# A new order for the down stages of a mixture-of-experts kernel: rows' sums, weights' pairs, output copies and gathers

## The chip, the cores and the metric

The kernel runs on one core of a Trainium2 chip. The metric is the device time of one execution in microseconds; the median of three runs is given. The engines are called TensorE (PE in the profile's rows; its weight loads are PEld), VectorE (DVE), ScalarE (ACT), GpSimd (POOL) and SyncE (SP, which only issues DMAs). A name like L1277 is a line of the kernel before.

## The reference

First comes causal attention with decay: 8 batches of 8 heads, 576 positions, 64 dimensions. Its output, as 4608 rows of 512 numbers, goes through a mixture of 8 experts. Each row is given to the expert with the largest gate logit; the expert computes `relu(x @ w1[e]) @ w2[e]` (512 to 1024 to 512), and the result is scaled by the row's gate weight and by a sigmoid of a second gate.

```
e_idx = argmax(x @ w_gate)
for e in range(8):
    rows = e_idx == e
    out[rows] = gate_w * eom[e] * (relu(x[rows] @ w1[e]) @ w2[e])
```

## The kernel before

The attention runs in the first 330 us by an order written out by hand; the change leaves it alone. Its rows go to DRAM as float16 upper and lower parts. The experts follow, in another hand-written order (`manual_schedule`): every engine runs its instructions in the order in which the code issues them. An instruction that waits holds up all that stands behind it on its engine.

**Numbers in two parts.** A float32 matrix is held as an upper float16 part and a lower part; a product is three matmuls: upper with upper, upper with lower, lower with upper.

**One expert.** Each expert has a fixed room for rows: two with 640, the others with 640, 608, 592, 576, 560 and 512 (`CAPS`). An expert has an up stage (`up_seven`) and a down stage (the loop over tiles at the end of `expert`'s code). The up stage multiplies by a seven-product scheme of Strassen's kind on halves: the weights are used as A11, A12, A22, S1, S2, S4, S3 and the rows as four quarters of `xT` and four sums T1 to T4. For each of four pairs `p` of weight blocks it forms products in three PSUM tiles: `y` (in a bank named `hp0`), `z` and `v` (banks `hp1`). A product that is used twice is first copied by ScalarE to `keep` (L1290), and the next product is then accumulated onto it in the same bank. VectorE adds the pieces (L1314, L1318, L1324); ScalarE and VectorE write the upper and the lower part of the hidden rows (`hh` L1282, `hl` L1284). The seventh product of the last pair (`finish_up`) runs inside the first tile of the down stage.

**The down stage** makes one output tile of 128 rows after another (`down_sum`, L1091 to L1093, 24 matmuls of 512 columns into a bank `y`; there are two such banks). ScalarE copies the bank, scaled, to `ys` (L1103), and GpSimd scatters `ys` to the output by an indirect DMA (L1107). A last tile with 96 rows or fewer is *narrow*: its matmuls take 64 or 32 rows side by side (`narrow_sum`, L1124), and VectorE adds the partial sums up (L1132, L1134; six instructions when it has both a 64-row and a 32-row part, two when it has 64 rows only).

**Prepared in the shadow of these stages, for the next expert:**

- The rows are gathered from DRAM by GpSimd's indirect DMAs (`gather_rows`, L816, one per tile of 128) and turned by DMA transposes on SyncE's queue (`gather_turn`, L822). Both are issued in `between`, which is called eight times in an up stage (`fc` 0 to 7).
- `between` also splits one W2 tile of this expert: ScalarE makes the upper part (L1009), GpSimd the lower part (L1010). It fetches the W2 tile four further on, and from `fc` 4 on tiles of the next W1 (L778).
- `rows_whole` adds upper and lower part of the turned rows to float32 (L1235): four GpSimd instructions over all columns, behind the up stage.
- `rows_sums` makes T1 to T4 for one half `k` of the contraction: VectorE subtracts into PSUM tiles in `hp1` (L1247), ScalarE casts the upper part (L1248), VectorE subtracts for the lower part (L1251). It is called in the second and the third tile of a down stage.
- `weights_pair` makes the seven blocks of one pair of W1: VectorE forms S1, S2, S4 (L1208, L1210, L1211) and two lower parts, GpSimd forms S3 in the tile `xr` (L1209) and three lower parts (L1206), ScalarE casts the upper parts (L1203). It is called in tiles 0, 1, 3 and 4, before that tile's output copy.

So on ScalarE the order within one tile is: sums (tiles 1 and 2), pair (all but tile 2), output copy of the tile.

**The hand-over** from attention to experts (from 349 us) is written out separately. The first expert (`W2`, `h`) has three tiles early and two (`xl`) later; in between, all of the second expert's rows are gathered and turned, its four W1 pairs are made without GpSimd (`first_splits`), and its sums follow the up stage of the two late tiles (L1065). On SyncE's queue the order is: transposes of `xl`, four fetches of W2 tiles, five transposes of `x1`. On the side engines: both halves of the sums, the last pair, then the two tiles with their copies.

## Time and profile before

| | us |
|---|---|
| median of 3 runs | 731.97 (728.39 to 734.08) |
| the profiled execution | 736.71 |
| its span, first to last instruction | 735.0 |
| TensorE busy | 690.8 |
| GpSimd busy | 554.6 |
| VectorE busy | 514.5 |
| ScalarE busy | 415.4 |

The profile is of one execution. Busy time leaves out the instructions that only wait, branch or issue a DMA. A wait of an engine is put down to the instruction, or the DMA, whose end came last before it went on.

The stages on this time line: attention to 330, hand-over to 386.5, then seven experts, each an up stage of 19 to 30 us and a down stage of 24 to 28 us, and an end of about 7 us after the last matmul.

### The profile page before, as it was taken

How to read it: one execution, taken by the hardware profiler on the slowest of the kernel's cores; microseconds unless marked ns; L12 is line 12 of the kernel's file. 1: busy time of each engine (PE TensorE's matmuls, PEld its weight loads, DVE VectorE, ACT ScalarE, POOL GpSimd, SP SyncE). 2: the span in 40 equal slices, each digit the busy share in tenths (PEclk: the TensorE clock that was granted, in tenths of full speed). 3: DMA queues.
4: the chain of work that ended last, by engine and by line, in shares of the span. 5: the costliest groups of instructions: out<-in, count | busy, mean ns of one | idle time of the engine just before them, and what ended most of it. 6: DMA issues, size and time to landing. Idle time of an engine off the chain costs nothing. (4 is left out here: it accounts for less than half of the span.)

```text
span 735.0 us, 22266 instructions
## 1 busy us (share of the span) xinstructions
PE 690.8 (94%) x8823; PEld 457.4 (62%) x8842; DVE 514.5 (70%) x1175; ACT 415.4 (57%) x990; POOL 554.6 (75%) x618
## 2 busy tenths in 40 slices
PE   4999999999999989989997999999989899889996
PEld 1577777777777767776464646547447356475664
DVE  7567798899889977876845575575585585656642
ACT  4456676667667645654425556566456465665641
POOL 8779799999989987862534768778767777788742
PEclk9999999999999999999998999999999999999999
DMA  4536666677797575265763934917819529366201
GB/s 153 162 115 175 176 169 168 167 170 165 191 178 188 158 164 140 61 139 179 195 127 93 220 124 121 273 60 171 225 46 207 195 69 246 130 145 230 76 15 40
DMA packets 119451, 110.71 MB, mean 151 GB/s; under 512 B 82669, under 2 KB 92077, under 8 KB 119344
## 3 DMA queue, kind: packets, MB, share of 16 engines
q1 hardware_dynamic: 108566, 71.50, 40.7%
q10 hardware_dynamic: 4618, 18.88, 8.6%
q0 software_dynamic: 6160, 18.88, 8.0%
q8 instruction: 70, 1.15, 0.7%
q14 instruction: 37, 0.30, 0.2%
HBM read 72.47 MB, written 19.49 MB: 125 GB/s over the span
## 5 line engine op out<-in xcount | busy, mean ns | idle before, releaser
L434 POOL TENSOR_TENSOR plo<-p 128x512 f16<-128x512 f32 x182 | 194.5, 1087 | 25.9 <-PE mx L305 12.7
L1277 PE MATMUL hp<-xT,sh 128*128 128x320 f16 (+5 forms) x784 | 150.8, 292 | 11.5 <-ACT keep L1290 7.9
L336 DVE TENSOR_REDUCE nR<-mx 128x2 f32<-128x1024 f32 (+4 forms) x154 | 121.2, 804 | 39.5 <-PE mx L305 37.2
L432 ACT ACTIVATE p<-sc 128x512 f32<-128x512 f32 x192 | 111.5, 595 | 65.3 <-PE sc L305 63.2
L305 PE MATMUL sc<-qk 64*128 64x64 f32 (+5 forms) x644 | 114.8, 435 | 0.0
L1277 PE MATMUL hp<-xT,sl 128*128 128x320 f16 (+5 forms) x392 | 114.4, 292 | 0.0
L1091 PE MATMUL y<-w2h,hh 128*128 128x512 f16 x272 | 103.1, 379 | 7.6 <-ACT ys L1103 7.6
L1093 PE MATMUL y<-w2h,hl 128*128 128x512 f16 x272 | 103.1, 379 | 1.0
L1277 PEld LDWEIGHTS <-sh 128*128 128x128 f16 x784 | 77.1, 99 | 39.1 <-issue 15.1
L1092 PE MATMUL y<-w2l,hh 128*128 128x512 bf16 x253 | 95.9, 379 | 0.0
L305 PEld LDWEIGHTS <-pick 64*128 64x128 bf16 (+1 forms) x1152 | 55.4, 98 | 56.2 <-issue 43.0
L1010 POOL TENSOR_TENSOR w2l<-w2r,w2h 128x512 bf16<-128x512 f32 x56 | 65.0, 1163 | 31.4 <-ACT w2h L1009 30.1
L505 PE MATMUL av<-Vs,p 128*128 128x65 f16 x640 | 65.8, 193 | 1.3 <-ACT xr L552 1.3
L1282 ACT ACTIVATE hh<-hp 128x320 f16<-128x320 f32 (+5 forms) x84 | 34.9, 417 | 56.2 <-DVE hp L1314 27.9
L506 PE MATMUL av<-Vs,p 128*128 128x64 bf16 x640 | 65.7, 195 | 0.0
L507 PE MATMUL av<-Vs,plo 128*128 128x65 f16 x640 | 65.4, 192 | 0.0
L305 PE MATMUL mx<-qk 64*128 64x512 bf16 (+3 forms) x372 | 55.4, 311 | 7.9 <-DMA qk<-in_qk_dram 5.6
L505 PEld LDWEIGHTS <-p 128*128 128x128 bf16 x640 | 59.1, 97 | 5.5 <-issue 5.3
L1284 DVE SCALAR_TENSOR_TENSOR hl<-hp,hh 128x320 f16<-128x320 f32 (+5 forms) x84 | 38.4, 458 | 33.7 <-ACT hh L1282 33.5
L506 PEld LDWEIGHTS <-p 128*128 128x128 bf16 x640 | 59.4, 97 | 1.4 <-issue 1.4
L507 PEld LDWEIGHTS <-plo 128*128 128x128 f16 x640 | 59.4, 99 | 0.0
L305 PE MATMUL mx<-Ek,Eq 63*128 63x512 f16 (+3 forms) x372 | 55.0, 299 | 2.9 <-DMA Ek<-d 2.9
(262 smaller groups left out, 1791.7 us busy)
## 6 DMA issues: line engine op xcount, KB each, us to landing
qk<-in_qk_dram ACTq DMA_DIRECT2D x31, 576.0 KB
w1r<-in_w_dram SPq DMA_DIRECT2D x64, 256.0 KB
w2r<-in_w_dram SPq DMA_DIRECT2D x64, 256.0 KB
v<-in_vm_dram SPq DMA_DIRECT2D x15, 576.0 KB
xbuf<-x SPq DMA_DIRECT2D x16, 512.0 KB
Eq<-mts SPq DMA_DIRECT2D x64, 0.1 KB
xbuf<-x SPq DMA_DIRECT2D x16, 64.0 KB
xT<-x SPq DMA_TRANSPOSE x62
```

The source lines that it names most:

```text
L305: nc.tensor.matmul(dst(i), w(i), x(i), start=start, stop=stop)
L336: nc.vector.tensor_reduce(o, x, axis=AX.X, op=ALU.max, negate=True)
L432: nc.scalar.activation(out=f32, in_=src, func=AF.Exp, scale=0.125)
L434: eng.tensor_tensor(lo, f32, upper(f32), op=ALU.subtract)
L505: nc.tensor.matmul(dst, ph, vv[:, 0:W], start=kc == 0, stop=False)
L506: nc.tensor.matmul(dst[:, 0:D], ph, vv[:, W:].bitcast(BF16), start=False, stop=False)
L507: nc.tensor.matmul(dst, pl, vv[:, 0:W], start=False, stop=kc == qc)
L1010: eng.tensor_tensor(l, raw, h, op=ALU.subtract)
L1091: nc.tensor.matmul(y, hh[:, fc, sl], wh, start=j == 0, stop=False)
L1092: nc.tensor.matmul(y, hh[:, fc, sl], wl, start=False, stop=False)
L1093: nc.tensor.matmul(y, hl[:, fc, sl], wh, start=False, stop=j == NF - 1)
L1277: nc.tensor.matmul(m, w[part][:, j, k], b(q, k), start=first and k == i == 0, stop=k == 1 and i == 2, skip_group_check=True)
```

## The change

In words:

- A narrow tile is the third of its down stage and not the last (order 0, 1, 4, 2, 3), and its sums use the banks `hp0`.
- The output copy of a tile is issued one tile later: after the next tile's matmuls and sums, ahead of its weights' pair. The pairs are made in positions 0, 2, 3 and 4.
- T3 and its lower part are made by GpSimd, in SBUF tiles `xr`, and T3 is the fourth of the sums before the lower parts start.
- `rows_whole` returns its adds as a list of steps. Two are run at `fc` 6 and two at `fc` 7 of the up stage, each time behind GpSimd's W2 split.
- The gathers come at `fc` 0, 0, 1, 1, 2 and the transposes at `fc` 1, 2, 2, 3, 4.
- In the first pair of an up stage A12's product comes before S2's.
- At the hand-over the four W2 fetches come after the transposes of `x1`; its adds are cut at column 384; the sums' halves alternate with the two late tiles.
- In the last down stage each copy is issued one tile later too.

```diff
     def narrow_sum(w2s, h, r0, n):
...
-        y = pm.tile([P, DM], F32, name="y", bufs=2)
+        y = staged(DM, "hp0")
...
-    def down_narrow(w2s, x, h, t, rest):
+    def narrow_sums(w2s, h, t, rest):
+        return [(narrow_sum(w2s, h, t * P + p0, n), n, p0) for p0, n in ((0, 64), (64, 32)) if p0 < rest]
+
+    def narrow_put(x, t, rest, parts):
         ys = m2.tile([P, DM], F32, name="ys", bufs=3)
-        for p0, n in ((0, 64), (64, 32)):
-            if p0 < rest:
-                y = narrow_sum(w2s, h, t * P + p0, n)
-                narrow_out(x, t, ys, y, n, p0)
+        for part in parts:
+            narrow_out(x, t, ys, *part)
         put_rows(ys[0:64 if rest <= 64 else 96], x, t)
...
-    def rows_whole(x, cap):
+    def rows_whole(x, cap, cuts=None):
...
-        for i in range(2):
-            for k in range(2):
-                nc.gpsimd.tensor_tensor(whole[i][:, k, 0:cap], xT[:, i, 0, k, 0:cap], xT[:, i, 1, k, 0:cap], op=ALU.add)
-        return whole, th, tl
+        def add(i, k, a, b):
+            nc.gpsimd.tensor_tensor(whole[i][:, k, a:b], xT[:, i, 0, k, a:b], xT[:, i, 1, k, a:b], op=ALU.add)
+        steps = [lambda i=i, k=k, a=a, b=b: add(i, k, a, b)
+                 for a, b in cuts or [(0, cap)] for k in range(2) for i in range(2)]
+        return (whole, th, tl), steps
...
-        def minus(j, x, y):
-            ts[j] = staged(n)
-            nc.vector.tensor_tensor(ts[j], x, y, op=ALU.subtract)
+        def minus(j, x, y, eng=nc.vector):
+            ts[j] = staged(n) if eng is nc.vector else ar.tile([P, 512], F32, name="xr")[:, 0:n]
+            eng.tensor_tensor(ts[j], x, y, op=ALU.subtract)
             nc.scalar.copy(out=th[:, j, k, 0:n], in_=ts[j])
-        def lower(j):
-            nc.vector.tensor_tensor(tl[:, j, k, 0:n], ts[j], th[:, j, k, 0:n], op=ALU.subtract)
+        def lower(j, eng=nc.vector):
+            eng.tensor_tensor(tl[:, j, k, 0:n], ts[j], th[:, j, k, 0:n], op=ALU.subtract)
         minus(T1, b12, b11)
         minus(T2, b22, ts[T1])
         minus(T4, b21, ts[T2])
+        minus(T3, b22, b12, nc.gpsimd)
         lower(T1)
-        minus(T3, b22, b12)
         lower(T2)
         lower(T4)
-        lower(T3)
+        lower(T3, nc.gpsimd)
...
             between(p, 0)
+            v = staged(n)
+            if p == 0:
+                product(v, w, A12, rows_of_half(1, 0), True)
             product(y, w, S2, rows_sum(T2), False)
             u2 = kept(2, y)
-            v = staged(n)
-            product(v, w, A12, rows_of_half(1, 0), True)
+            if p:
+                product(v, w, A12, rows_of_half(1, 0), True)
...
                 table_weights(x1[0], 1, 0, CT)
-                W2r = [fetch_w2(w2[1], k) for k in range(AHEAD)]
...
             gather_rows(x1, t)
             gather_turn(x1, t)
+        W2r = [fetch_w2(w2[1], k) for k in range(AHEAD)]
...
-        sums = rows_whole(x1, CAP)
+        sums, adding = rows_whole(x1, CAP, [(0, EARLY), (EARLY, CAP)])
+        for f in adding:
+            f()
         up(W1, x, [(EARLY, CAP)], h)
-        for k in range(2):
-            rows_sums(sums, CAP, k)
-        first_splits(3, HF)
-        down(W2, xl, h, ET, CT)
+        for t in range(ET, CT):
+            y = down_sum(W2, h, t)
+            rows_sums(sums, CAP, t - ET)
+            if t == CT - 1:
+                first_splits(3, HF)
+            down_out(xl, y, t)
...
-                    if fc < nt:
-                        gather_rows(x1, fc)
-                    if 2 <= fc < 2 + nt:
-                        gather_turn(x1, fc - 2)
+                    for t in ((0, 1), (2, 3), (4,))[fc] if fc < 3 else ():
+                        if t < nt:
+                            gather_rows(x1, t)
+                    for t in ((0,), (1, 2), (3,), (4,))[fc - 1] if 1 <= fc < 5 else ():
+                        if t < nt:
+                            gather_turn(x1, t)
...
+                    if fc == 6:
+                        sums_n.extend(rows_whole(x1, nx["cap"]))
+                    for f in sums_n[1][2 * fc - 12:2 * fc - 10] if fc >= 6 else ():
+                        f()
...
-            if nx:
-                sums_n = rows_whole(x1, nx["cap"])
-            for t in range(tiles):
-                if nx is None and t == tiles - 1:
-                    down_halves(W2, x, h, t)
+            todo = None
+            for pos, t in enumerate((0, 1, 4, 2, 3) if SM < cap <= SM + 96 else range(tiles)):
+                if nx is None and pos == tiles - 1:
+                    todo()
+                    todo = lambda t=t: down_halves(W2, x, h, t)
                     continue
                 rest = cap - t * P
-                y = down_sum(W2, h, t, None if t else finish_up) if rest > 96 else None
+                if rest > 96:
+                    y = down_sum(W2, h, t, None if pos else finish_up)
+                    out_ = lambda y=y, t=t: down_out(x, y, t)
+                else:
+                    out_ = lambda parts=narrow_sums(W2, h, t, rest), t=t, rest=rest: narrow_put(x, t, rest, parts)
                 if nx:
-                    for g in PAIRS[2 * t + AHEAD:2 * t + AHEAD + 2]:
+                    for g in PAIRS[2 * pos + AHEAD:2 * pos + AHEAD + 2]:
                         W1r[g] = fetch_w1(m2, nx["w1"], g, 8)
-                    if t in (1, 2):
-                        rows_sums(sums_n, nx["cap"], t - 1)
-                    if t != 2:
-                        W1n.append(weights_pair(W1r, len(W1n)))
-                    if t == 3:
+                    if pos in (1, 2):
+                        rows_sums(sums_n[0], nx["cap"], pos - 1)
+                    if pos == 3:
                         W2r = [fetch_w2(nx["w2"], fc) for fc in range(AHEAD)]
-                if y is None:
-                    down_narrow(W2, x, h, t, rest)
-                else:
-                    down_out(x, y, t)
+                if todo:
+                    todo()
+                todo = out_
+                if nx and pos != 1:
+                    W1n.append(weights_pair(W1r, len(W1n)))
...
+            todo()
```

## Rows read from the trace of the kernel before

**Rows 1.** The page: busy us and share; then one group, busy, mean ns | idle before.
```profile
PE 690.8 (94%) x8823; PEld 457.4 (62%) x8842; DVE 514.5 (70%) x1175; ACT 415.4 (57%) x990; POOL 554.6 (75%) x618
...
L1010 POOL TENSOR_TENSOR w2l<-w2r,w2h 128x512 bf16<-128x512 f32 x56 | 65.0, 1163 | 31.4 <-ACT w2h L1009 30.1
```
**Rows 2.** TensorE's waits after 386 us: who <- whom: us, times, longest.
```profile
PE hp L1277 <- ACT keep L1290: 7.9, 7, 3.1
PE y L1091 <- ACT ys L1103: 7.6, 7, 1.7
PE hp L1277 <- DVE y L1324: 2.4, 2, 1.2
```
**Rows 3.** Timeline, TensorE, hand-over: start, us, instruction, count, [idle before <- ended by].
```profile
388.75 0.43 PE L1277 MATMUL hp<-xT,sh 128*128 128x320 f16 x2 [1.23 <-DVE xT L1251]
...
392.81 0.69 PE L1277 MATMUL hp<-xT,sh 128*128 128x320 f16 x2 [3.08 <-ACT keep L1290]
```
**Rows 4.** Busy by stretch: PE, PEld, DVE, ACT, POOL, clock, DMA share, GB/s.
```profile
392.80:398.60 5.80, 5.79 (x22) 3.29 (x22) 1.22 (x3) 1.86 (x5) 3.58 (x4) 0.50 0.44 144
```
**Rows 5.** Busy by stretch, the same columns: two down stages, 608 and 576 rows.
```profile
515.31:542.90 27.59, 25.76 (x150) 11.70 (x149) 18.68 (x39) 14.13 (x33) 19.65 (x21) 1.00 0.57 165
615.40:642.08 26.68, 24.48 (x127) 11.15 (x126) 16.43 (x39) 13.88 (x33) 18.45 (x19) 1.00 0.61 183
```
**Rows 6.** Timeline, TensorE, a tile's start in the first of these stages.
```profile
533.51 0.38 PE L1091 MATMUL y<-w2h,hh 128*128 128x512 f16 x1 [1.73 <-ACT ys L1103]
533.73 0.38 PE L1092 MATMUL y<-w2l,hh 128*128 128x512 bf16 x1
```
**Rows 7.** Timeline, ScalarE, the same stage.
```profile
525.39 0.40 ACT L1203 CAST sh<-xr 128x256 f16<-128x256 f32 x1 [4.06 <-POOL xr L1209]
```
**Rows 8.** Timeline, VectorE, the same stage: first, waiting and last instructions.
```profile
519.08 0.42 DVE L1208 TENSOR_TENSOR hp<-w1r 128x256 f32<-128x256 f32 x1
...
526.78 0.47 DVE L1247 TENSOR_TENSOR hp<-x,hp 128x296 f32<-128x296 f32 x1 [3.26 <-ACT xT L1248]
...
543.76 1.02 DVE L1206 TENSOR_TENSOR sl<-hp,sh 128x512 bf16<-128x512 f32 x2 [0.65 <-ACT sh L1203]
...
547.03 2.32 DVE L1134 SCALAR_TENSOR_TENSOR ys<-y,idsr,ys 32x512 f32<-32x512 f32 x3
```
**Rows 9.** Timeline, SyncE's issues at the hand-over.
```profile
357.58 2.57 SPq L1003 DMA_DIRECT2D w2r<-in_w_dram  x4
```
**Rows 10.** Timeline, GpSimd, the whole rows' adds at the hand-over.
```profile
376.16 5.70 POOL L1235 TENSOR_TENSOR x<-xT 128x640 f32<-128x640 f16 x4 [8.31 <-DMA xT<-xg]
```
**Rows 11.** Timeline, GpSimd: the fifth gather, and the adds in two down stages.
```profile
509.31 1.02 POOL L816 DMA_INDIRECT xg<-xbuf,idsr  x1 [0.16 <-PE hp L1277]
...
519.29 5.37 POOL L1235 TENSOR_TENSOR x<-xT 128x592 f32<-128x592 f16 x4 [1.81 <-DVE hl L1284]
...
620.27 5.05 POOL L1235 TENSOR_TENSOR x<-xT 128x560 f32<-128x560 f16 x4 [2.69 <-DMA xT<-xg]
```
**Rows 12.** Timeline, VectorE, hand-over: the sums' start, a wait, the last pair's end.
```profile
377.58 1.68 DVE L1247 TENSOR_TENSOR hp<-x 128x320 f32<-128x320 f32 x1 [0.36 <-POOL x L1235]
...
380.54 0.50 DVE L1247 TENSOR_TENSOR hp<-x,hp 128x320 f32<-128x320 f32 x1 [1.28 <-POOL x L1235]
...
391.02 1.28 DVE L1206 TENSOR_TENSOR sl<-hp,sh 128x512 bf16<-128x512 f32 x2
```
**Rows 13.** Durations by line, whole trace: ns min/median/max, first and last start.
```profile
L1209 POOL TENSOR_TENSOR xr<-w1r x24: 721/750/1028, 423.7 to 688.8; 128x256 f32<-128x256 f32 x24
...
L1247 DVE TENSOR_TENSOR hp<-x x28: 433/638/1675, 377.6 to 681.6; 128x320 f32<-128x320 f32 x8, 128x304 f32<-128x304 f32 x4, 128x296 f32<-128x296 f32 x4, 128x288 f32<-128x288 f32 x4
L1247 DVE TENSOR_TENSOR hp<-x,hp x28: 428/471/497, 380.5 to 680.8; 128x320 f32<-128x320 f32 x8, 128x304 f32<-128x304 f32 x4, 128x296 f32<-128x296 f32 x4, 128x288 f32<-128x288 f32 x4
```
**Rows 14.** Timeline, ScalarE, hand-over: output copies and first products kept.
```profile
391.17 1.28 ACT L1103 ACTIVATE ys<-y,idsl 128x512 f32<-128x512 f32 x2
392.32 0.77 ACT L1290 COPY keep<-hp 128x320 f32<-128x320 f32 x2
```

More of the change, by code (lines that the diff above doesn't have):

```diff
@@ L1456, in between @@
                         W1r[g] = fetch_w1(m2, nx["w1"], g, 8)
+                    if fc == 6:
+                        sums_n.extend(rows_whole(x1, nx["cap"]))
+                    for f in sums_n[1][2 * fc - 12:2 * fc - 10] if fc >= 6 else ():
+                        f()
+            sums_n = []
             finish_up = up_seven(W1, x, sums, cap, h, between)
             W1n, W2n = [], []
-            if nx:
-                sums_n = rows_whole(x1, nx["cap"])
-            for t in range(tiles):
-                if nx is None and t == tiles - 1:
-                    down_halves(W2, x, h, t)
+            todo = None
@@ L1477, in _attn_moe @@
-                if y is None:
-                    down_narrow(W2, x, h, t, rest)
-                else:
-                    down_out(x, y, t)
-                if nx is None and t == 0:
+                    if pos in (1, 2):
+                        rows_sums(sums_n[0], nx["cap"], pos - 1)
+                    if pos == 3:
+                        W2r = [fetch_w2(nx["w2"], fc) for fc in range(AHEAD)]
+                if todo:
[3 more added lines that the diff above has]
+                    W1n.append(weights_pair(W1r, len(W1n)))
@@ L1482, in _attn_moe @@
+                if nx is None and pos == 0:
                     ncum = overflow_slots()
-                if nx is None and t == tiles - 2:
+                if nx is None and pos == tiles - 2:
                     nsl = nc.values_load(ncum, min_val=0, max_val=(NT - min(CAPS)) // P + E)
+            todo()
             if nx:
-                e, x, W1, W2, sums = nx, x1, W1n, W2n, sums_n
+                e, x, W1, W2, sums = nx, x1, W1n, W2n, sums_n[0]
     with tc.For_i(0, nsl, 1) as i:
```

## The prediction

> **What bounds the kernel now.** I read the page's first part, then TensorE's waits, busy time by stretch, and timelines around them. TensorE is busy 690.8 of 735.0 us [rows 1], so only its idle time can be won. What the change touches starts at about 350 us. From 386 us on TensorE's waits sum to 19.1 us in 17 pieces [rows 2, 3]: 7.9 until ScalarE has copied a first product to `keep`, 7.6 until ScalarE has emptied an output bank (`ys`), 2.4 until VectorE has read `y`, 1.2 until it has written a sum's lower part. Two of them stand together at the hand-over, 1.23 and 3.08 us [rows 3], and behind these the granted clock is 0.50, the lower level of 1.2 GHz, for 5.8 us [rows 4]: 2.9 us more. Elsewhere a wait of 1.73 us leaves the clock at 1.00 [rows 5, 6]. So there are three pots: hand-over 7.2 us, output banks 7.6, stage starts 7.2 (4.8 `keep` without the hand-over's, and 2.4). Together 22.0.
>
> What makes these waits: in a down stage (one is the first row of [rows 5]) the three side engines work through fixed queues: GpSimd four adds for the whole rows, then its part of a weights' pair; ScalarE waits 4.06 us for GpSimd's `xr` [rows 7], VectorE 3.26 us for ScalarE behind that [rows 8], and TensorE for an output copy queued behind both [rows 6].
>
> **The change, part by part.** The sum is made against the profiled execution, 736.7 us with 735.0 of span; the median of the runs is 731.97, 4.7 lower, so I subtract the same microseconds from the median.
>
> *Hand-over.* Four W2 fetches hold SyncE's queue from 357.58 to 360.15 [rows 9], ahead of the five transposes, and GpSimd stands 8.31 us, to 376.16, until the last has landed [rows 10]. Behind the transposes, the fetches free 2.6 us: rows at 373.6 or sooner. The W2 tiles are first split behind `keep`, at about 388, so that fetching them some 12 us later than now, after the transposes, costs nothing. Eight adds for four: 640 columns take 1.43 each and 560 take 1.26 [rows 10, 11], so 2.0 ns a column and 0.13 fixed; four more cost 0.5 us, and those of the first three tiles run before the last rows land. All end near 376.5, before VectorE's first sum at 377.58. VectorE's chain, 377.58 to 392.30 [rows 12], loses a stretch (1.68 for about 0.5: 1.2), a wait of 1.28, and four T3 instructions (two subtractions, two lower parts, some 0.45 each by the 433 to 497 ns of [rows 13]: 1.8): 4.3, so it ends near 388.0. ScalarE's `keep` follows that end closely (392.32 against 392.30 [rows 12, 14]), TensorE 0.5 later: 388.5. TensorE itself arrives at 392.81 - 1.23 - 3.08 [rows 3] plus A12's product, six times 0.13: 389.3. ScalarE now does one `ys` (0.64 [rows 14]) in the middle of the sums, and `v` takes the bank of the last pair's sum; I leave 0.7 for both. Without 4.3 us of idle time the clock stays up. **Saved 6.5** (bounds: 0 if the rows come no sooner; 7.2).
>
> *Output copies one tile later, ahead of the pair.* Tile k's copy now stands behind the sums of tile k+1 only, and its bank is needed at tile k+2 (later still where the narrow tile, in `hp0`, lies between). The pair before it is finished a whole tile earlier. **Saved 7.6** (bounds 0 and 7.6). What is late next is the stage's end.
>
> *Stage starts.* Take the stage with 608 rows whose successor has 592. VectorE's queue runs from 519.08 to 549.35 [rows 8]. Of that, T3 goes to GpSimd: 1.8 us for both halves. The wait of 3.26 shrinks. GpSimd's adds begin at 519.29, when the last rows are in [rows 11]; the fifth gather, issued at 509.31 behind five splits of W2, is now behind three, some 2.6 us sooner. That gives rows at 516.7, two adds to 519.4, the eighth split (1.16 [rows 1]) to 520.5, two adds to 523.2, against 524.66: 1.5 sooner. The `ys` that stood ahead of T1's cast (0.6) is out of the way too: 2.1. So VectorE ends at 549.35 - 1.8 - 2.1 = 545.4. Its last work is now the fourth pair, not the narrow tile's six instructions (0.77 each); from the pair's last subtraction to its end are 0.65 + 1.02 [rows 8], so that subtraction is done at 543.7. Behind it ScalarE does two casts (1.0), the `xr` cast (0.3), the last `ys` (0.6) and `keep` (0.4) [rows 7, 14]: 546.0. TensorE gets there at 542.90 [rows 5] - 1.73 [rows 6] + 2.3 (three products of six at 0.13) = 543.5. A wait of 2.5 stays. The 592 stage is alike: 5.0 stay in these two. With 48 or 64 rows in the narrow tile VectorE has four narrow instructions fewer (3.1 us [rows 8]), and TensorE 24 products, four side by side in 0.216 [rows 6]: 1.3; that leaves 2.5 - 3.1 + 1.3 = 0.7 at most, and with the shorter rows there I take 0.4, twice. After five whole tiles VectorE has no narrow work, and nothing stays. **Saved 7.2 - 5.8 = 1.4** (bounds: 0, all 7.2). The `y` wait goes, since the narrow tile no longer stands ahead of the first adds; if it did not, 2.4 return.
>
> *T3 on GpSimd* appears nowhere in the trace. Its nearest rows are `xr<-w1r`, 256 columns in 0.72 to 1.03 us [rows 13], and VectorE's own, 433 at the least [rows 13]. Four a stage at about 0.8 are 3.2 us for an engine that is busy 19.7 of 27.6 us there [rows 5]; it covers them, unless ScalarE stands for T3's cast. I take 0.7 over all stages for that, and 0.6 for the two adds now ahead of the eighth split: 1.3 (bounds 0, and the last rival).
>
> VectorE's subtraction of two SBUF operands takes 433 to 1675 ns, the one with a PSUM operand never over 497 [rows 13]. The Trainium skill (SBUF — State Buffer, Who interferes with whom) says that a VectorE instruction with two SBUF inputs and a GpSimd instruction that reads SBUF block each other. By that rule, with which the trace agrees, T3's move has a price: if one T1 a stage stands behind a T3, an estimated 0.8, the two long stages lose 1.6 more, and the sum would be 12.6 and the time 719.4. I keep the sum without it, since VectorE's rows before hold such stretches already.
>
> The rest I cost at nothing. The gathers put in pairs hold the second and third W2 splits back by a gather each on GpSimd, and the transposes hold the W2 fetches back on SyncE; both run ahead of need, since the splits are first read in the next stage. The last expert's copies and register load move where TensorE has no wait [rows 2]; A12's product first is counted above.
>
> Sum: 6.5 + 7.6 + 1.4 - 1.3 = **14.2**. The profiled 736.7 becomes 722.5, the median 717.8.
>
> **Rivals.**
> *The side engines are the bound.* What TensorE no longer waits for in mid-stage it waits for at the next start: saved are the hand-over's 6.5 and the T3 instructions, some 1.5 in all: 724. For it: exactly that happens in my two long stages. Against: VectorE is busy 18.7 of 27.6 us [rows 5], and most of the rest is waiting on the chain that the change loosens. Chance 0.20, half of it above 724.7.
>
> *The hand-over stays late*, that is, its reordering does not do what it says: if gathers, not W2, hold the transposes, adds still begin at 376 and 5 of the 6.5 are lost: 722.8. For it: the fetches explain 2.6 of the 18.6 between 357.58 and 376.16. Chance 0.10.
>
> *Slower: whole-row adds hold back the eighth split of W2.* It is needed by the first tile's 23rd product, 5.7 us into the stage (22 x 0.216 [rows 6], 6 x 0.13 [rows 3] between), and now stands behind two adds (2.7) and takes 1.16 itself: rows that land later than 1.8 us into the stage stop TensorE. Now they land 4.0 (519.29 against 515.31) and 4.9 (620.27 against 615.40) into it [rows 5, 11]; by my working the first comes at 1.4. If they stayed at 4.9 in all six stages, each would lose 3.1 and hand the sums on 1.2 later: 4.3 x 6 = 26, so 744. Against it: the gather does leave two splits sooner. Chance 0.07.
>
> **How the numbers follow.** The forecast has 0.63, by itself 710 to 723. The low end is everything saved, 22 us: 710, less a little for the runs' spread. The high end takes in the rivals at 722.8 and 724, the latter with half of its spread: 727. From no change a measurement tells 1%, 7.3 us: faster than 724.7 are the forecast less 0.05, the hand-over rival and half of the first: 0.78; slower 0.07; within 1% 0.15.
>
> **What would show it.** Right: no `y` <- `ys` waits of TensorE, clock 1.00 past the hand-over with under 1 us of waits there, GpSimd's adds in two pairs around the eighth split, `keep` waits of 2 to 3 us at two stage starts and none elsewhere. Wrong: `y` waiting for `w2l`, waits of 1 to 3 us at all starts, ScalarE standing for T3, or the adds still waiting for transposes at 376.

## The result, and the profile after

The changed kernel takes 724.56 us (median of 20 runs, 719.94 to 729.11). The kernel before, run beside it, takes 735.05 us (20 runs, 728.39 to 741.52). The ratio is **0.9871, 95% interval 0.9846 to 0.9895**: 1.3% faster. The forecast was 717.8 us, 1.9% faster, in a range from a little under 710 to 727. The direction held; a third of the expected gain didn't come.

The profiled execution took 727.22 us (span 725.5). It is 9.5 us shorter than the profiled execution of before, but the two can't be compared as they stand. The experts' first down tile, up to which the change alters nothing, starts at 350.14 us in that profile and at 346.60 here. The kernel before, profiled once more (before_again, below), starts it at 346.39. So I compare the part from this tile's start to the last matmul: 378.1 us before, 377.9 in the second profile of it, **372.7 after**.

TensorE's waits in this part (who waits <- for whom: us in total, times, longest). Before, profiled again, with the same three groups as [rows 2]:

```profile
PE hp L1277 <- ACT keep L1290: 7.9, 7, 3.1
PE y L1091 <- ACT ys L1103: 7.8, 6, 1.7
PE hp L1277 <- DVE y L1324: 2.4, 2, 1.2
PE hp L1277 <- DVE xT L1251: 0.8, 1, 0.8
```

After:

```profile
PE y L1092 <- POOL w2l L1010: 5.5, 2, 4.4
PE hp L1281 <- DVE sl L1207: 3.9, 5, 2.0
PE hp L1281 <- ACT keep L1294: 3.7, 3, 1.3
PE y L1091 <- ACT ys L1103: 0.3, 1, 0.3
```

The waits for `ys` are gone, and so are those for `y`. A new one heads the list: a down tile that waits for `w2l`, the lower part of a W2 tile, which GpSimd makes. It was the prediction's rival on the slow side, in two of the six stages.

**The hand-over.** After, TensorE's timeline (start, duration, instruction, count, idle before and what ended it) and busy time by stretch (stretch, length, the five engines as in [rows 4], then the granted clock, the DMA share and GB/s), and then GpSimd's timeline:

```profile
385.35 0.43 PE L1281 MATMUL hp<-xT,sh 128*128 128x320 f16 x2 [0.56 <-DVE sl L1207]
```

```profile
386.30:392.10 5.80, 5.80 (x45) 4.20 (x43) 3.04 (x7) 3.96 (x10) 5.19 (x5) 1.00 0.29 85
```

```profile
364.93 6.01 POOL L1236 TENSOR_TENSOR x<-xT 128x384 f32<-128x384 f16 x8 [0.62 <-DMA xT<-xg]
```

Of the 1.23 and 3.08 us of [rows 3] 0.56 is left, and the clock stays at 1.00 where [rows 4] had 0.50. The eight adds of the whole rows begin 18.3 us behind the first down tile (364.93 - 346.60), against 26.0 in [rows 10] (376.16 - 350.14), and GpSimd stands 0.62 us for them, not 8.31. The first four of them need only the rows of the first three tiles. SyncE's last transpose there ends 17.8 us behind the first down tile (364.41) against 23.7 and 23.3 in the two profiles of before (373.80 and 369.73), so the last rows come 5.5 to 5.9 us sooner.

**The start of a stage.** After the down stage of 608 rows, TensorE, and the clock behind it:

```profile
529.54 0.41 PE L1281 MATMUL hp<-xT,sh 128*128 128x296 f16 x2 [0.33 <-DVE sl L1207]
...
532.46 0.41 PE L1281 MATMUL hp<-xT,sh 128*128 128x296 f16 x2 [2.00 <-DVE sl L1207]
...
534.59 0.65 PE L1281 MATMUL hp<-xT,sh 128*128 128x296 f16 x2 [1.21 <-ACT keep L1294]
```

```profile
534.40:538.00 3.60, 3.41 (x15) 2.04 (x15) 0.66 (x2) 1.69 (x5) 3.34 (x4) 0.53 0.19 73
```

3.54 us of waiting in three pieces, and behind them 3.60 us at a clock of 0.53, the lower level of 1.2 GHz. What makes it is seen on VectorE and ScalarE just before:

```profile
521.77 0.73 DVE L1132 TENSOR_SCALAR ys<-hp,idsr 64x512 f32<-64x512 f32 x1
...
524.11 2.32 DVE L1134 SCALAR_TENSOR_TENSOR ys<-hp,idsr,ys 32x512 f32<-32x512 f32 x3
...
526.46 0.43 DVE L1209 TENSOR_TENSOR hp<-w1r 128x256 f32<-128x256 f32 x1
```

```profile
527.85 0.86 ACT L1204 CAST sh<-hp 128x512 f16<-128x512 f32 x2 [5.65 <-DVE hp L1212]
```

VectorE works through the narrow tile's six instructions ahead of the third pair of weights, while ScalarE stands 5.65 us for that pair. The third and the fourth pair then run into the next up stage, whose first products need the banks that the fourth pair's sums hold. GpSimd is held up too: its scatter of the narrow tile stands ahead of its part of the third pair, and so ScalarE gets the fourth pair's `xr` late. GpSimd, then ScalarE:

```profile
527.02 0.96 POOL L1107 DMA_INDIRECT out_dram<-ys,idsr  x1 [3.76 <-DVE hp L1209]
```

```profile
533.25 0.40 ACT L1204 CAST sh<-xr 128x256 f16<-128x256 f32 x1 [1.29 <-POOL xr L1210]
```

**The new wait.** GpSimd in a later stage (576 rows, its down stage from 601.96), SyncE's issues, and TensorE:

```profile
592.88 1.00 POOL L816 DMA_INDIRECT xg<-xbuf,idsr  x1 [0.31 <-issue]
...
608.27 2.44 POOL L1236 TENSOR_TENSOR x<-xT 128x560 f32<-128x560 f16 x2 [6.90 <-DMA xT<-xg]
610.66 1.33 POOL L1010 TENSOR_TENSOR w2l<-w2r,w2h 128x512 bf16<-128x512 f32 x1
```

```profile
602.82 3.24 SPq L822 DMA_TRANSPOSE xT<-xg  x2
```

```profile
612.05 0.58 PE L1092 MATMUL y<-w2l,hh 128*128 128x512 bf16 x1 [4.43 <-POOL w2l L1010]
```

The fourth gather is issued at 592.88; its transpose starts at 602.82, 9.9 us later. GpSimd stands 6.90 us for the transposed rows with the eighth W2 split behind the two adds, and TensorE stands 4.43 us for that split. The gather's own row lasts 1.00 us. The Trainium skill (Perfetto Trace Analysis, DMA Instruction — SWDGE (GPSIMD)) says that the end which a profile gives for such a DMA of GpSimd is the end of making its descriptors and not of moving the data; the trace agrees, 1.00 against 9.9 us.

### The profile page after: what moved, and what is told of

Same layout as the page of the kernel before. It is cut to its first block, busy times and chain, and to the rows that moved or that the text cites. A ratio compares the mean times of both kernels' runs of the same rounds, so it can differ in the third digit from the quotient of the medians.

```text
span 725.5 us, 22266 instructions
## 1 busy us (share of the span) xinstructions
PE 688.8 (95%) x8823; PEld 456.5 (63%) x8842; DVE 506.6 (70%) x1147; ACT 415.9 (57%) x990; POOL 574.4 (79%) x650
## 3 DMA queue, kind: packets, MB, share of 16 engines
q8 instruction: 70, 1.15, 0.7%
```

## Experiments

Each kernel was timed in five rounds beside the kernel before; ratios are to it. Edits are to the changed kernel unless said. "Waits" are TensorE's from the hand-over on. "D" is the start of a down stage.

**e1_adds_behind**: all four adds behind the eighth split.

```diff
-                    for f in sums_n[1][2 * fc - 12:2 * fc - 10] if fc >= 6 else ():
+                    for f in sums_n[1] if fc == 7 else ():
```

> All four whole-row adds behind the eighth W2 split, else the changed kernel. My theory: TensorE's 5.5 us of waits for w2l come from the adds that stand ahead of that split; they vanish, the adds begin no later than where the rows land, and the first half's sums come at most 1.2 us later: 0 to 4 us less than the changed kernel, ratio to the kernel before 0.982 to 0.987. Rival: the side engines' chain sets the stage's end, so each microsecond that the sums come later returns as a keep wait at the next stage's start: ratio 0.987 to 0.991.

Measured 725.48 us, ratio 0.9862 (0.9814 to 0.9911).

```profile
PE hp L1281 <- ACT keep L1294: 4.9, 4, 1.3
...
PE y L1091 <- ACT ys L1103: 3.1, 2, 1.7
```

The `w2l` waits are gone, so they do come from the adds ahead of the split. The time stays: the adds now begin at D + 2.1 to 2.8 in all six stages. GpSimd stands for no rows there; it is the place behind the eighth split that sets their start, as it does in the first two stages of the kernel before (D + 2.1 and 2.4). The sums come later, and 3.1 us of `ys` waits return, in these two stages. What is won at the split is lost at the banks.

**e2_single_gathers**: the order of gathers and transposes as before.

```diff
-                    for t in ((0, 1), (2, 3), (4,))[fc] if fc < 3 else ():
...
+                    if fc < nt:
+                        gather_rows(x1, fc)
+                    if 2 <= fc < 2 + nt:
+                        gather_turn(x1, fc - 2)
```

> Gathers and transposes at the old steps (one a step, transposes two steps later), the adds still ahead of the eighth split. My theory: the pairs bring the rows some 2.6 us sooner; without them rows land 4 to 5 us into the stage, w2l waits of 2 to 3 us stand in at least four stages, 10 us in all: ratio to the kernel before 0.996 to 1.002. Rival: gathers in pairs collide with the transposes on the DMA engines and land late by that; singles land as soon: w2l waits of 6 us or less in all, ratio 0.984 to 0.990.

Measured 735.04 us, ratio 0.9993 (0.9956 to 1.0030).

```profile
PE y L1092 <- POOL w2l L1010: 6.4, 4, 3.5
PE hp L1281 <- DVE sl L1207: 4.9, 4, 2.0
PE y L1091 <- ACT ys L1103: 4.0, 2, 2.1
PE hp L1281 <- ACT keep L1294: 2.8, 3, 1.2
```

Without the sooner gathers the whole change is worth nothing that can be told from noise. Rows that land late hurt twice: the eighth split (6.4) and the sums, whose copies come late (4.0).

**e3_old_handover**: the hand-over as before.

```diff
+                W2r = [fetch_w2(w2[1], k) for k in range(AHEAD)]
...
+        sums, adding = rows_whole(x1, CAP)
...
+        for k in range(2):
+            rows_sums(sums, CAP, k)
+        first_splits(3, HF)
+        down(W2, xl, h, ET, CT)
```

> The hand-over as in the kernel before (W2 fetches ahead of the transposes, four uncut adds, both halves of the sums and the last pair ahead of the two late tiles), with T3 on GpSimd and the rest of the change. My theory: the hand-over is worth 6.5 us; about 4 us of waits and a stretch at half clock come back: ratio to the kernel before 0.994 to 0.998. Rival: T3 on GpSimd alone frees VectorE's chain there, the reordering is worth 2 us or less: ratio 0.987 to 0.990.

Measured 726.18 us, ratio 0.9889 (0.9824 to 0.9953): 1.3 us more than the changed kernel, with an interval of 5 us to either side. In the trace the first up stage takes 27.3 us to its down stage, against 22.7 after and 29.5 and 29.1 in the two profiles of before. The trace shows 4.6 us; the time can't confirm the size. The theory's range (0.994 to 0.998) is missed and the rival's (0.987 to 0.990) holds the median, so by time alone the reordering may be worth 2 us or less.

**e4_t3_on_vector**: T3 and its lower part on VectorE again.

```diff
-        minus(T3, b22, b12, nc.gpsimd)
         lower(T1)
+        minus(T3, b22, b12)
...
-        lower(T3, nc.gpsimd)
+        lower(T3)
```

> T3 and its lower part back on VectorE, else the changed kernel. My theory: VectorE has 1.8 us more in each of six down stages and at the hand-over; the two stages with a long narrow tile lose 1.8 each, the hand-over about 1, the others little: 4 to 6 us, ratio to the kernel before 0.992 to 0.995. Rival: GpSimd is what the stages wait for; without four more instructions a stage its chain ends sooner: ratio 0.980 to 0.986.

Measured 729.69 us, ratio 0.9927 (0.9889 to 0.9965): T3's place is worth some 4 us (0.0056 of 735).

```profile
PE hp L1281 <- DVE sl L1207: 8.1, 5, 2.0
```

The waits for `sl` grow from 3.9 to 8.1: the end of VectorE's queue is what the next up stage starts on.

**e5_narrow_last**: the narrow tile last, as before.

```diff
-            for pos, t in enumerate((0, 1, 4, 2, 3) if SM < cap <= SM + 96 else range(tiles)):
+            for pos, t in enumerate(range(tiles)):
```

> The narrow tile last again, in the banks hp0 and with its copy issued last, else the changed kernel. My theory: its place is worth little by itself. Ahead of the last two pairs its six VectorE instructions hold those pairs up (some 4.6 us in two stages); behind them they hold up the first adds of the next up stage, so keep waits shrink and the y wait of about 1.2 us comes back in two or three stages: ratio to the kernel before 0.986 to 0.992. Rival: its place is what removed the waits at the stages' starts; without it 5 us or more return: ratio 0.993 to 0.999.

Measured 722.85 us, ratio 0.9838 (0.9787 to 0.9889); the changed kernel's 0.9871 lies in this interval. The waits move: those for `sl` fall to 0.6 and those for `keep` go, but 6.0 for `ys` and 3.0 for the narrow tile's own `ys` come. The narrow tile's place is worth nothing that these runs tell; its six VectorE instructions cost about the same wherever they stand. The 6.0 us for `ys` matter below: in the 608 stage the adds begin at D + 1.3 both here and in the changed kernel, yet here TensorE stands 1.57 us for `ys` and there none. A copy that is a tile late still holds a bank too long; the narrow tile in the middle, which uses no `y` bank, gives it the time.

**e6_defer_alone**: the kernel before with the copies one tile later, and nothing else. The pairs stay in tiles 0, 1, 3 and 4, so that the copy of tile 1 stands behind the second pair and one half of the sums; in the changed kernel that pair comes behind the copy.

```diff
...
-                    if t != 2:
-                        W1n.append(weights_pair(W1r, len(W1n)))
...
-                if y is None:
-                    down_narrow(W2, x, h, t, rest)
-                else:
-                    down_out(x, y, t)
+                if todo:
+                    todo()
+                todo = out_
+                if nx and t != 2:
+                    W1n.append(weights_pair(W1r, len(W1n)))
...
+            todo()
```

> The kernel before with one part of the change alone: each output copy is issued one tile later, ahead of that tile's pair. My theory: the ys waits (7.6 us) go, but GpSimd's and VectorE's chains are as long as before, so that about half comes back as keep waits at the next stage's start: ratio to the kernel before 0.993 to 0.997. Rival one: all of it comes back, 0.998 to 1.002. Rival two: nothing comes back, 0.988 to 0.991.

Measured 748.12 us, ratio 1.0196 (1.0145 to 1.0246): **2% slower than before**.

```profile
PE y L1091 <- ACT ys L1103: 26.2, 12, 3.6
```

One down stage (from 463.14): GpSimd's adds, ScalarE, then TensorE's waits:

```profile
465.26 5.40 POOL L1235 TENSOR_TENSOR x<-xT 128x608 f32<-128x608 f16 x4
```

```profile
479.81 0.41 ACT L1248 CAST xT<-hp 128x304 f16<-128x304 f32 x1 [1.64 <-DVE hp L1247]
...
483.00 1.27 ACT L1103 ACTIVATE ys<-y,idsr 128x512 f32<-128x512 f32 x2
```

```profile
475.65 0.38 PE L1091 MATMUL y<-w2h,hh 128*128 128x512 f16 x1 [1.18 <-ACT ys L1103]
...
483.74 0.38 PE L1091 MATMUL y<-w2h,hh 128*128 128x512 f16 x1 [2.75 <-ACT ys L1103]
```

Every theory missed this. Two copies are issued back to back at 483.00, behind the second pair and the four casts of the second half, which wait for VectorE's sums. The rows are not what is late here: the adds begin at D + 2.1 without a wait. With two banks, a copy that is a tile late leaves no slack: `ys` waits go from 7.8 to 26.2 us. Of these, 11.8 stand at the third tiles, whose bank is freed by a copy in the place that the change gives it; 14.4 stand at the fourth, whose copy has the second pair ahead of it here and not in the change. So e6 isn't quite the step to which the prediction had given 7.6 us of gain, but 11.8 us of waits stand where the order is the same.

**e8_split8_on_vector**: the eighth split's lower part on VectorE.

```diff
-                W2.append(split_w2(W2r[fc], nc.gpsimd))
+                W2.append(split_w2(W2r[fc], nc.vector if fc == NF - 1 else nc.gpsimd))
```

> The eighth W2 tile's lower part made by VectorE instead of GpSimd, so that the whole-row adds stand ahead of nothing that the first tile needs; else the changed kernel. My theory: the w2l waits (5.5 us in the profile) go, nothing else is late for it, and GpSimd has 1.2 us less a stage: 3 to 6 us less than the changed kernel, ratio to the kernel before 0.979 to 0.984. Rival: the stages' ends are set by the sums and pairs, which still wait for the rows; what the first tile gains comes back at the next stage's start: 0.986 to 0.990.

**e9_split8_and_narrow_act**: e8, and the narrow tile's first scaled copy on ScalarE.

```diff
-        nc.vector.tensor_scalar(dst, y[0:n], w, None, op0=ALU.mult)
+        nc.scalar.activation(out=dst, in_=y[0:n], func=AF.Copy, scale=w)
```

> As the kernel with the eighth split on VectorE, and besides the first of a narrow part's instructions (the scaled copy out of the bank) on ScalarE. My theory: VectorE has 1.5 us less in the two stages with a 64- and a 32-row part and 0.75 in the two with a 64-row part; the keep and bank waits at the next starts shrink by that and the stretch at half clock behind one of them goes: 3 to 5 us less than with the split alone, ratio to the kernel before 0.973 to 0.979. Rival: ScalarE's casts of the pairs come later by as much, no change against the split alone.

Measured 721.84 us, ratio 0.9831 (0.9776 to 0.9886), and 720.92 us, ratio 0.9820 (0.9770 to 0.9869). The waits of e9:

```profile
PE hp L1281 <- ACT keep L1294: 4.4, 4, 1.2
PE hp L1281 <- DVE y L1331: 3.1, 4, 1.2
PE hp L1281 <- DVE sl L1207: 1.8, 2, 1.2
```

Neither `w2l` nor `ys` is left: the split no longer waits for rows, and the adds still run early. A new wait of 3.1 us for `y` stands in its place, since the last product of the up stage now waits for an addition behind the split on VectorE. The part from the first down tile to the last matmul takes 365.2 us, 7.5 less than after. Both are faster than the two kernels by their medians; against the changed kernel, 0.5%, the intervals overlap. The ratio of e8 is in its theory's range; that of e9 is not, and its 0.9 us against e8 can't be told from nothing, as its rival said.

**e10_copies_at_once**: each copy behind the sums and the pair of its own position, as before.

```diff
...
-                if todo:
-                    todo()
-                todo = out_
                 if nx and pos != 1:
                     W1n.append(weights_pair(W1r, len(W1n)))
+                out_()
...
```

> The changed kernel with each tile's output copies issued at once, behind the sums and the pair that follow that tile's call, as the kernel before does; gathers in pairs, adds ahead of the eighth split and the hand-over stay as changed. e6 showed that copies one tile later cost 2% on the kernel before, where rows come late. Theory (with rows sooner and the pair behind the copy, the late copies do pay: ScalarE no longer stands for the end of a tile ahead of the next sums and casts): waits of TensorE for ys come back at 2 to 5 us, time 0.990 to 0.994 of before. Rival (the late copies are worth nothing or cost here too, and the whole gain of the ys waits is the rows'): waits for ys at 0 to 1.5 us, 0.980 to 0.987.

Measured 726.89 us, ratio 0.9901 (0.9866 to 0.9936).

```profile
PE hp L1281 <- DVE sl L1207: 6.8, 5, 1.7
PE y L1092 <- POOL w2l L1010: 6.0, 3, 3.3
PE hp L1281 <- ACT keep L1294: 3.9, 4, 1.3
```

No wait for `ys`, although the copies are issued as before: the theory's mechanism falls. In the last three of the six stages the adds begin late (D + 2.8 to 5.2) and TensorE stands for `w2l` instead; in the first three (D - 0.4 to -0.9) neither wait is there. Its time would fit, and the rival's doesn't, but the interval also holds the changed kernel's. The late copies are worth between nothing and some 5 us here.

**e12_rows_alone**: the kernel before with the rows sooner, and with the adds ahead of the eighth split. As in the changed kernel, two adds stand behind the seventh split and two behind the eighth.

```diff
...
+                    for t in ((0, 1), (2, 3), (4,))[fc] if fc < 3 else ():
...
+                    if fc == 6:
+                        sums_n.extend(rows_whole(x1, nx["cap"]))
+                    for f in sums_n[1][2 * fc - 12:2 * fc - 10] if fc >= 6 else ():
+                        f()
...
```

> The kernel before with the rows sooner alone: gathers in pairs, their transposes at once, and the whole rows' adds two ahead of the seventh and two ahead of the eighth W2 split; the copies, the sums by the tile, the pairs of weights, the order of the tiles and the hand-over are those of before. Theory (rows that are there when the sums ask for them are what took the ys waits away): waits for ys under 3 us (7.6 before), 0.990 to 0.996 of before. Rival (the rows alone bring nothing without the finer order of sums, pairs and copies): waits for ys stay at 5 us or more, 0.998 to 1.004.

Measured 728.54 us, ratio 0.9927 (0.9891 to 0.9963).

```profile
PE hp L1280 <- ACT keep L1293: 6.1, 5, 3.1
PE y L1092 <- POOL w2l L1010: 5.6, 2, 4.2
PE hp L1280 <- DVE xT L1254: 3.9, 1, 3.9
...
PE y L1091 <- ACT ys L1103: 0.7, 2, 0.5
```

By its numbers the theory holds: the `ys` waits go from 7.8 to 0.7 us with the old copies, pairs and tile order. The stages tell how. In the first three the adds begin at D - 0.7 to -0.9 (2.1 to 3.7 in the second profile of before), and 3.4 us of `ys` waits become 0.2 with nothing in their place. In the stages of 592 and 576 rows they begin at D + 3.3 and 6.3 (4.1 and 5.6 before); there 4.5 us of `ys` waits become 0.5, but TensorE stands 5.6 us for `w2l`, the waits of the eighth split. So a sooner start of the adds is shown to take the waits away in three stages. It comes of two things at once, the gathers and the adds' place ahead of the split, and neither was tried alone on the kernel before.

**e11_best**: e9 with the eighth split behind the up stage's last addition, and the last copy of a down stage behind the next stage's first `keep`.

```diff
...
+                if fc == 0:
+                    while late:
+                        late.pop()()
+                if fc < NF - 1:
+                    W2.append(split_w2(W2r[fc], nc.gpsimd))
...
+            W2.append(split_w2(W2r[NF - 1], nc.vector))
...
+            if nx:
+                late.append(todo)
...
```

> e9 (eighth split's lower part on VectorE, the narrow tile's first scaled copy on ScalarE) with two more moves: the eighth split is issued behind the up stage's seven, so behind u's last add on VectorE, and the last output copy of a down stage is issued in the next up stage behind its first keep. Theory: the waits for y at the last product of the up stage (3.1 us in e9) go, those for keep at its start (4.4 us in four) get shorter by about 0.7 us each: 0.974 to 0.980 of before. Rival (the split now comes later than the first down tiles want it, or the copy's bank is wanted at once, so waits only change their name): 0.981 to 0.986, with waits of y for w2l, or of a product for ys, of 2 us or more.

Measured 721.23 us, ratio 0.9834 (0.9790 to 0.9877): the rival.

```profile
PE y L1091 <- ACT ys L1103: 3.6, 3, 2.2
PE hp L1281 <- DVE sl L1207: 3.1, 4, 1.2
PE hp L1281 <- ACT keep L1294: 2.8, 5, 0.7
```

The waits for `y` go and those for `keep` shrink to 0.7 at the longest, as the theory said, but waits for `ys` come and those for `sl` grow, by as much. e9 stays the best version by its median; e5, e8, e9 and e11 can't be told apart.

**before_again**: the kernel before, unaltered.

> The kernel before, unaltered, once more under a profile, to see how far one profile of it stands from the next. Theory: the attention part, which no kernel here alters, ends at 343 to 347 us as in the other profiles rather than at the 350.14 us of the profile that the prediction used, and the expert part from the first down tile to the end of the halves takes 376 to 381 us (378.1 there). Rival (350 us is this kernel's own): the attention part ends at 349 us or later. The ratio is 0.996 to 1.004 in any case.

Measured 733.91 us, ratio 0.9995 (0.9965 to 1.0025). Its waits stand in the section above: the same to 0.2 us in three groups of four. The first down tile starts at 346.39 us and the part behind it takes 377.9 us. The theory holds, and the 350.14 us of the first profile is that execution's own.

## Why the prediction was right in its sign and too large

Step by step, in the profile after against the second profile of before. TensorE's own loss at the lower clock is counted as half of the stretch.

| step | predicted | shown by the traces |
|---|---|---|
| hand-over | 6.5 saved | 0.84 + 3.09 of waits and 3.0 of clock before, 0.56 after: 6.4 saved |
| output copies | 7.6 saved | 7.8 to 0.3: 7.5 saved, but not by the copies' place alone |
| stage starts | 1.4 saved | 7.2 of waits before; 7.0 and 1.7 of clock after: 1.5 lost |
| T3 and the eighth split | 1.3 lost | 5.5 of waits and 2.1 of clock: 7.6 lost |
| sum | 14.2 | 4.8 |

The part from the first down tile on shrank by 5.2 us (377.9 to 372.7), so the waits and the clock account for it. The medians give 10.5 us and the ratio 9.5. (The forecast of 717.8 started from a median of 731.97; beside the changed kernel the kernel before took 735.05, so 3.1 of the 6.8 us between 717.8 and 724.56 are the start's.) This profiled execution lies 2.7 us above its median and the second one of before 1.2 below: with these 3.9 the 5.2 become 9.1. Where an average execution of the changed kernel saves the 4 us that this one lost isn't shown; the `w2l` waits, which vary with the landing of the rows, are the likely place.

**Hand-over: right, by the trace.** The fetches' place, the halves in between and T3 together gave what the sum said, and the clock stayed up; the times of e3 are too wide to confirm it. On the side engines more was won than I worked out: the last transpose ends 5.5 to 5.9 us sooner, not 2.6.

**Output copies: right in size, wrong in cause.** This step failed as the prediction put it ("Tile k's copy now stands behind the sums of tile k+1 only, and its bank is needed at tile k+2"). It left out that the copy then waits for whatever those sums wait for. With the rest as before, later copies cost 14 us (e6, 1.96% of 735). With the copies at once and the adds begun sooner, the `ys` waits are 0.7 in the old order (e12) and 0 in the new (e10); with the copies late and the adds begun at D + 1.5 to 2.2, they are there in the two stages of 640 rows, by whatever cause the adds are late: the order in e1 (3.1), the rows in e2 (4.0). So what took the waits away is that the sums start sooner, through the gathers and the adds' place together; the size came out by luck. Two reserves stand beside that. In the stages where the rows still land late, a wait for `w2l` stands where that for `ys` stood (e10, e12, and the 576 stage after). And the late copies need the narrow tile between, as the prediction's bracket ("later still where the narrow tile, in `hp0`, lies between") had it: without it 6.0 us are back, 5.0 of them in the stages that have such a tile (e5).

The prediction counted the sooner gathers in the stage starts alone (1.5 us), and at the banks not at all. Their worth by the runs:

| | order of before | the rest of the change |
|---|---|---|
| gathers as before | 1 | 0.9993 (e2) |
| gathers in pairs | 0.9927 (e12) | 0.9871 |

In the right column only gathers and transposes differ: they are worth 9 us there. In the left column the adds stand ahead of the eighth split in e12 and behind it in the kernel before, so its 5 us are of both together. All the rest is worth 0.5 us without the gathers and about 4 with gathers and adds in place.

**Stage starts: mis-sized.** The waits for `y` went, as said, and `keep` has shrunk from 4.8 to 3.7, but 3.3 us of waits for `sl` are new. At the 608 stage 3.54 us stay, not 2.5, and the clock falls behind them, which the sum had at nothing: 1.7 us. Two of the other starts have 1.75 and 1.76 where I had 2.5 and 0.4, and the last has none. The sum had VectorE's queue right: it runs for 26.4 us in the 608 stage (506.34 to 532.74), and 519.08 to 545.4 are 26.3. What it left out is GpSimd's queue. It put the cast of `xr` straight behind VectorE's last subtraction; ScalarE stood 1.29 us for `xr` there, because GpSimd had stood 3.76 us until VectorE was past the narrow tile. That covers the 1.0 us by which the wait is longer. The rival "the side engines are the bound" put 724, near the measured 724.56, but by another road: it had the banks' 7.6 us come back at the starts. Of these 1.5 came back there; 7.6 were lost at the eighth split, in this execution. That the two numbers meet is chance.

**The eighth split: the rival's mechanism, in two stages.** I priced it for all six stages or for none. Its point was that rows landing later than D + 1.8 us stop TensorE. (Its 22 x 0.216 and 6 x 0.13 make 5.5 us, not 5.7; the trace has the split needed at 607.62, D + 5.7.) GpSimd's adds begin at D + -0.7, -0.9, 1.3, 0.4, 6.3 and 3.1 in the six stages after. The first four have no wait; the last two have 4.43 and 1.05, where start less 1.8 gives 4.5 and 1.3. In e10 the late stages' adds begin at D + 3.7, 5.2 and 2.8 and wait 1.91, 3.33 and 0.77; in e2, at 2.2, 2.3, 3.6 and 5.3, the four waits sum to 6.4, by the rule 6.2. So the point was right and the rows' landing was not. I let the sooner fifth gather carry over 2.6 us in full, and in the 576 stage it carried over nothing (D + 4.9 before, [rows 5, 11], 6.3 after). Behind the 4.43 us the clock falls too:

```profile
612.00:616.20 4.20, 4.15 (x10) 1.43 (x10) 2.15 (x4) 1.51 (x4) 4.20 (x4) 0.50 0.98 349
```

**T3's price.** The prediction weighed the Trainium skill (SBUF — State Buffer, Who interferes with whom) at 1.6 us. T1 on VectorE, the subtraction of two SBUF operands, after (ns min/median/max):

```profile
L1251 POOL TENSOR_TENSOR xr<-x x14: 721/816/881, 370.9 to 667.6; 128x320 f32<-128x320 f32 x4, 128x304 f32<-128x304 f32 x2, 128x296 f32<-128x296 f32 x2, 128x288 f32<-128x288 f32 x2
L1251 DVE TENSOR_TENSOR hp<-x x14: 421/830/1276, 373.6 to 665.2; 128x320 f32<-128x320 f32 x4, 128x304 f32<-128x304 f32 x2, 128x296 f32<-128x296 f32 x2, 128x288 f32<-128x288 f32 x2
```

T3 on GpSimd takes 816 ns, the 0.8 of the estimate. The second row is T1 alone; in e4 the row holds T3 as well. Taken alone, T1's mean is 770 ns after, 647 in e4, and 766 and 821 in the two profiles of before. The stretch is plain where T1 of the second half runs beside T3's lower part on GpSimd, as at the hand-over, after and then in e4:

```profile
377.24 0.94 DVE L1251 TENSOR_TENSOR hp<-x 128x320 f32<-128x320 f32 x1
```

```profile
377.22 0.49 DVE L1251 TENSOR_TENSOR hp<-x 128x320 f32<-128x320 f32 x1
```

Three of the 14 run so for most of their time: 916 to 935 ns, against 476 to 493 for the same three in e4. That agrees with the rule, and costs 1.3 us over the whole run where the estimate had 1.6 in the two long stages. It doesn't decide: with it paid, T3's move is still worth some 4 us. That the stretch comes from GpSimd's reads and not from something else in the stage no run here isolates.

## What to carry to other kernels

When an engine's copy waits behind other work in a fixed queue, ask first what that work waits for: starting that work sooner removed the waits here, while moving the copy behind it made them three times as long. A step that is counted for one wait alone can be the one that takes another away, so follow its product to the last wait that it feeds. When a wait disappears, look in the same stage for one that has taken its place. When a needed instruction is put behind work that waits for a DMA, work out the landing time at which it stops the critical engine, and do it stage by stage, not for all or none.

## What the runs showed of the hardware

- **Landing of a gather.** The same gather of 128 rows was followed by its transpose 3.4 to 6.4 us after its issue in the first four stages after the change, and 9.9 us after it at 592.88 us, where the mean busy share of the DMA engines is 0.95 to 1.15 for 12 us (as the profile counts it, it can pass 1) while the bytes moved fall:

```profile
592.00:598.00 6.00, 6.00 (x51) 4.79 (x50) 3.67 (x10) 4.40 (x13) 5.48 (x6) 1.00 0.95 178
598.00:604.00 6.00, 5.95 (x43) 4.12 (x43) 2.93 (x7) 2.80 (x8) 2.81 (x3) 1.00 1.15 144
```

  The kernel before has shares of 1.00 to 1.18 in its stage with the same rows (608 to 620 us) and transposes 3.4 to 4.6 us after the gathers, so the share alone doesn't explain it. In this stage the adds begin at D + 4.7 to 6.3 after and in e3, e5, e10, e11 and e12, but at D + 3.2 in e9, 0.7 in e4 and 0.5 in e8. Why is left open.
- **The lower clock** (0.53 and 0.50) came behind 3.54 us of waits in three pieces, as it did before behind 4.3 us in two pieces at the hand-over [rows 3, 4], and behind a single wait of 4.43.
- **One profile is one execution.** In 14 profiles of kernels that share everything up to the first down tile, that tile starts between 342.9 and 350.1 us. A sum made against one profile's whole span carries these 7 us.
